# First batch's running sums added by broadcast from its third tile on; the short tile's parts in nine blocks; padding and zeros off GpSimd

## The chip, the cores and the metric

The kernel runs on one core of a Trainium2 chip. TensorE (PE), VectorE (DVE), ScalarE (ACT) and GpSimd (POOL) each run their own instruction list in order; SyncE (SP) and POOL also issue transfers. The metric is the device time of one execution in microseconds (us), as the median of several runs. Tiles of 128 rows live in on-chip memory (SBUF); PE writes into eight banks of accumulators (PSUM).

## The reference, cut to what matters

```
def _attn_ref(q, k, v, s):            # 4 batches, 8 heads, 576 tokens, head size 64
    scores = scale * np.matmul(q, k.transpose(0, 1, 3, 2))
    cum = np.cumsum(np.maximum(s, 0.0), axis=-1)
    bias = -(cum[:, :, :, None] - cum[:, :, None, :])
    scores = np.where(causal, -1e9, scores + np.minimum(bias, 0.0))
    scores = scores - np.max(scores, axis=-1, keepdims=True)
    attn = np.exp(scores)
    attn = attn / (np.sum(attn, axis=-1, keepdims=True) + 1e-09)
    return np.matmul(attn, v)

x = attention, as 2304 tokens x 512
h = x @ w1_in;  x = (h * tanh(softplus(h))) @ w1_out      # 512 -> 2048 -> 512
h = x @ w2_in;  out = (h * sigmoid(1.702 * h)) @ w2_out
```

In a row of scores the part of the bias that belongs to the query is a constant, which the softmax removes. What has to be added to a score is the running sum `cum` of its key.

## The kernel before, in words

**Work.** Each batch of 576 tokens is cut into five query tiles: `i` = 0 to 3 with 128 rows and the short tile `i` = 4 with 64. A step (`steps`, 26 of each batch, 104 in all) makes the scores of one tile for a few heads: four heads for `i` = 0, two for `i` = 1, one for `i` = 2 (width `L` = 384) and `i` = 3 (512). In the short tile a step takes two heads, one in each half of the 128 rows, and cuts its 576 columns into two pieces of 288. The eight heads are in two groups `g` of four. While attention goes on, PE also works off the first layer (`h`, 256 tokens at a time): `first_layer` calls `tick` between its products, and each `tick` emits one step. The first layer for 256 tokens can begin when their attention is done; so there are stretches in which PE has only attention to do.

**Scores and sums.** `do_qk` makes a step's scores on PE in a tile `s`, two products for each head (q split in two parts `qw`, against `kw`) and one with a mask. In batches 1 to 3 the sums come from `ck` (tiles of 128 rows, all four heads of a group; filled by `load_ck` from `cum_d` in memory, the same line to every row, in two pieces) or, for the short tile, from `ckp` (named `cp`, filled by `load_ckp` into the same buffer as `ck`). `do_max` adds them on DVE while it takes the row minimum and leaves the result in `P`; `do_exp` is the exponential on ACT, from `P` to `P`. In batch 0 the sums come by PE: one product more for each head and piece, of a one-hot matrix `oneh` and the sums in three bf16 parts `cumb`; then `early_soft` takes the minimum on DVE straight from `s` and ACT does the exponential from `s`. `cum_split` makes the columns of `cumb`.

**Attention times v.** In batches 1 to 3 `do_hilo` splits `P` into two f16 parts in a tile `hl` (three buffers) which a transposing transfer on SP's queue turns into `pt`, and `do_av` multiplies block by block, two products for each block of 128 keys (the first part against both parts of v, the second part against the first part of v). The short tile has 576 columns, so that its fifth block has 64 keys; `do_hilo` fills it up to 128 with zeros by a POOL memset, and there are ten blocks to transpose. In batch 0 `early_pt` and `early_av` do the same on PE in f32.

**Preparing.** `load_group` (transfers issued by POOL) brings k, q and v of the next group as `kraw`, `qraw`, `vraw`; ACT makes a second copy of k and q (`twice`); `qT`, `kT`, `v1` and `v2` of `split_items` make `qw`, `kw` and v's two parts. The short tile's `qw` must be zero in half its columns: POOL's memset of the whole tile does that, once its buffer (two of them) is no longer read by PE. At the start SP fetches the sixteen pieces of `w1_in` (`fetch_a`, tiles `wst`), which `turn_w` splits later with ACT, DVE and POOL.

**Order.** The code's order is a request; a scheduler decides each engine's list from its own estimates, so a change in one place can move instructions elsewhere. Within a list nothing overtakes. All arithmetic helpers pass through line 76, so the trace is read by tile names.

Of the kernel before, what the change touches and what calls it, by code (L numbers as in the profile page):

```python
# [89 lines left out]
def attention_moe_moe_kernel(  # L90
# [118 lines left out]
    def load_group(b, i, g, dup=True):  # L209
        n = min(128, S - 128 * i)  # L210
        r = []
        for src, nm in ((k, "kraw"), (q, "qraw"), (v, "vraw")):
            if nm == "vraw" and b == 0:
                v_load(i, g, nc.gpsimd)
                continue
            w = 1 if nm == "vraw" else 2
            t = pp.tile([128, HG, w, D], F32, tag=nm, name=nm, bufs=2 if nm == "qraw" else 3)
            held(nc.gpsimd.dma_start(out=t[:n, :, 0, :], in_=rows(src, b, i, g)))
            if w == 1:
                t = t[:, :, 0, :]  # L220
            elif dup:
                twice(t, n)
            r.append(t)
        raw[b, i, g] = r
# [31 lines left out]
    def split_items(b, i, g):  # L256
# [13 lines left out]
        def qT():  # L270
# [5 lines left out]
            if pair:  # L276
                nc.gpsimd.memset(w.bitcast(F32), 0.0)
# [8 lines left out]
        def v1():  # L286
            if b not in vsc:
                vscale_set(b)
            vr = raw[b, i, g][2]
            vt[b, i, g] = vv = v_p.tile([128, HG, 2, D], F16, tag="v", name="v")  # L290
            nc.scalar.activation(out=vv[:n, :, 0, :], in_=vr[:n], func=AF.Copy, scale=vsc[b][:n, 0:1])

        def v2():
            vv = vt[b, i, g]
            nc.vector.scalar_tensor_tensor(
                out=vv[:n, :, 1, :], in0=raw.pop((b, i, g))[2][:n], scalar=vsc[b][:n, 0:1], in1=vv[:n, :, 0, :],
                op0=ALU.mult, op1=ALU.subtract,
            )
# [146 lines left out]
    def early_soft(x):  # L445
# [5 lines left out]
        sg = segs(x)  # L451
        if len(sg) == 1:
            ps = x["S"][0]
            low(mx[:, 0:mu], ps[:, 0:mu * L].rearrange("p (e l) -> p e l", e=mu))
            for e in range(mu):
                o = slice(e * L, (e + 1) * L)
                lut(
                    p[:, o], ps[:, o], AF.Exp, bias=mx[:, e:e + 1], scale=-1.0, accum_out=ts["sums"][:, j + e, 0:1]
                )
            return  # L460
        for f, (c0, c1) in enumerate(sg):
            low(mx[:, f:f + 1], x["S"][f][:, 0:c1 - c0])
        low(mx[:, 2:3], mx[:, 0:2])
        sm = sm_p.tile([128, 2], F32, tag="sm2", name="sm2")
        for f, (c0, c1) in enumerate(sg):
            lut(
                p[:, c0:c1], x["S"][f][:, 0:c1 - c0], AF.Exp, bias=mx[:, 2:3], scale=-1.0, accum_out=sm[:, f:f + 1]
            )
        nc.vector.tensor_reduce(out=ts["sums"][:, j, 0:1], in_=sm, axis=mybir.AxisListType.X, op=ALU.add)
# [44 lines left out]
    def do_qk(x):  # L514
        b, i, g, n, L = x["b"], x["i"], x["g"], x["n"], x["L"]
        x["S"] = []
        for c0, c1 in segs(x):
            ps = ps_s.tile([128, 512], F32, tag="s", name="s")
            x["S"].append(ps)
            for e, hs in enumerate(x["hs"]):  # L520
                o = ps[:, e * L:e * L + c1 - c0]
                for a, h in enumerate(hs):
# [6 lines left out]
                    if b == 0:  # L529
                        m = n if len(hs) == 2 else 128  # L530
                        nc.tensor.matmul(
                            out=o[64 * a:64 * a + m], lhsT=oneh[:, h:h + 1].to_broadcast([128, m]),
                            rhs=cumb[:, c0:c1], start=False, stop=c1 < L, skip_group_check=True,
                        )
# [31 lines left out]
    def do_hilo(x):  # L566
        L, mu, nb = x["L"], x["mu"], x["nb"]
        Lp = nb * 128
        w = mu * Lp
        hl = pp.tile([128, 2 * NTIL * 128], F16, tag="hl", name="hl", bufs=HLB)  # L570
        hv = hl[:, 0:2 * w].rearrange("p (a w) -> p a w", a=2)
        if Lp != L:
            nc.gpsimd.memset(hv[:, :, L:Lp], 0.0)
        wl = mu * L
        nc.scalar.activation(out=hv[:, 0, 0:wl], in_=x["P"][:, 0:wl], func=AF.Copy, scale=PSC)
        nc.vector.scalar_tensor_tensor(
            out=hv[:, 1, 0:wl], in0=x["P"][:, 0:wl], scalar=PSC, in1=hv[:, 0, 0:wl], op0=ALU.mult, op1=ALU.subtract
        )
        x["T"] = d = pt_p.tile([128, 2 * NTIL, 128], F16, tag="pt", name="pt")
        last_pt[0] = nc.sync.dma_start_transpose(out=d[:, 0:2 * mu * nb, :], in_=hl[:, 0:2 * w])  # L580
# [4 lines left out]
    def do_av(x):  # L585
        b, i, g, n, mu, nb = x["b"], x["i"], x["g"], x["n"], x["mu"], x["nb"]
        t = x["T"]
        for e, hs in enumerate(x["hs"]):
# [5 lines left out]
            for kb in range(i + 1):  # L594
                kn = min(128, S - 128 * kb)
                for a, h in enumerate(hs):
                    hl = h - g * HG
                    rows = slice(64 * a, 64 * a + n) if two else slice(0, 128)
                    vv = vt[b, kb, g][:kn, hl, :, :].rearrange("p c d -> p (c d)")
# [4 lines left out]
                    nc.tensor.matmul(  # L604
                        out=o[rows, j % 4, 0:D], lhsT=t[:kn, (mu + e) * nb + kb, rows], rhs=vv[:, 0:D],
                        start=False, stop=(kb == i), skip_group_check=True,
                    )
# [79 lines left out]
    def tick():  # L687
# [15 lines left out]
        if t < NS:  # L703
            do_qk(x)
            if x["b"]:
                do_max(x)
                do_exp(x)
            else:
                early_soft(x)
            if last_of[gi] == t and gi in late_k:  # L710
                late_k.pop(gi)()
            if last_of[gi] == t and x["i"] == LK // 128 - 1 and x["b"]:
# [135 lines left out]
    while fq:  # L848
        fetch_a()
    early_turn(0, 0)  # L850
# [11 lines left out]
    cum_split(256, S)  # L862
# [564 lines left out]
```

## Time and profile before

| | |
|---|---|
| median of 3 runs (lowest, highest) | 1020.62 us (1016.22, 1021.12) |
| the profiled execution: its own time, its span | 1023.25 us, 1021.2 us |
| PE busy | 981.8 us, 96% of the span |
| DVE, ACT, POOL busy | 668.9, 552.7, 269.4 us |
| batch 0 | until about 133 us |
| batches 1 to 3 | until about 415 us |
| the rest (second half of layer one, layer two) | until the end |

The profile is one execution; its times are in microseconds from the start of the span. "Clock" is the share of TensorE's full speed that was granted: 1.0 is 2.4 GHz, 0.5 is 1.2 GHz. A row of the timeline gives the start, the duration, and in brackets the idle time ahead of it with what ended it. A matmul's duration includes its way through the array, so that neighbours overlap: what a matmul costs is read from one start to the next.

### The profile page before, as it was taken

To read this page: it belongs to the slowest core of one execution; us is meant where nothing else is said; L and a number is where in the kernel's file an instruction comes from. 1 tells how busy PE (TensorE), PEld (TensorE's weight loads), DVE (VectorE), ACT (ScalarE), POOL (GpSimd) and SP (SyncE) were. 2 spreads that over 40 slices of the span, in tenths; PEclk is the share of its full clock that TensorE was granted. 3 is DMA by queue.
4 is the path that set the end of the run, shared out by engine and by line. 5 is a ranking of instruction groups with operands and counts; after the bars stand their busy time and mean duration, and the time that the engine had idled before them with its cause. 6 is when DMAs were issued, how large, how long until landed. Compare 5 with 4: busy or idle time off the path is not lost.

```text
span 1021.2 us, 20117 instructions
## 1 busy us (share of the span) xinstructions
PE 981.8 (96%) x7967; PEld 870.5 (85%) x7970; DVE 668.9 (66%) x1323; ACT 552.7 (54%) x1070; POOL 269.4 (26%) x332
## 2 busy tenths in 40 slices
PE   6899999989998999999999999999999999999997
PEld 5787797978987888998888888988888888888886
DVE  5777567666465787487997995994643653653553
ACT  4675377666565887387655763753433433433331
POOL 3543332234113311000000000054434333243331
PEclk9798999999999999999999999999999999999999
DMA  9644258999589979799997553400100100000000
GB/s 260 203 127 119 74 129 159 234 209 177 132 191 199 210 146 189 238 337 357 369 336 267 181 202 134 159 8 1 63 22 1 42 22 2 22 22 1 21 9 34
DMA packets 153773, 143.16 MB, mean 140 GB/s; under 512 B 91216, under 2 KB 122448, under 8 KB 153680
## 3 DMA queue, kind: packets, MB, share of 16 engines
q1 hardware_dynamic: 147456, 124.05, 45.0%
q0 software_dynamic: 6224, 17.83, 6.6%
q8 instruction: 62, 1.02, 0.4%
q14 instruction: 31, 0.25, 0.1%
HBM read 89.61 MB, written 32.58 MB: 120 GB/s over the span
## 4 chain that ended last, share of the span: by engine, by line
PE 63%; DMA 2%; DVE 1%; ACT 0%; issue 0%; DVEq 0%; SPq 0%
PE acc L76 24%; PE h L76 21%; PE p L76 16%; DMA pt<-hl 2%; PE s L76 1%; PE o L76 1%; DVE w2l L76 0%; PE xt L76 0%; PE qt L76 0%; PE kt L76 0%; DVE z L76 0%; DVE w2d L76 0%; DVE o L76 0%; DVE f L76 0%; ACT P L76 0%
## 5 line engine op out<-in xcount | busy, mean ns | idle before, releaser
L76 PE MATMUL h<-x,w2i 128*128 128x256 f16 x1728 | 199.9, 273 | 0.9 <-DVE z L76 0.9
L76 PE MATMUL h<-xh,w 128*128 128x256 f32 x1344 | 197.3, 296 | 1.5 <-ACT xh L76 1.0
L76 PEld LDWEIGHTS <-w2i 128*128 128x128 f16 x1728 | 169.1, 98 | 20.6 <-issue 1.1
L76 PE MATMUL acc<-gh,w 128*128 128x512 f32 (+1 forms) x640 | 181.7, 369 | 0.0
L76 PEld LDWEIGHTS h<-xh,w 128*128 128x128 f32 x1344 | 174.3, 196 | 5.5 <-ACT xh L76 1.9
L76 PE MATMUL p<-w2l,gh 128*128 128x256 f16 x504 | 136.0, 273 | 0.0
L76 PE MATMUL p<-w2h,gl 128*128 128x256 f16 x504 | 135.9, 273 | 0.0
L76 PEld LDWEIGHTS acc<-gh,w 128*128 128x128 f32 x640 | 116.1, 189 | 20.4
L76 PE MATMUL p<-w2h,gh 128*128 128x256 f16 x504 | 133.3, 273 | 0.2 <-DVE e L76 0.2
L76 PE MATMUL acc<-gl,w 128*128 128x512 f32 (+1 forms) x320 | 117.9, 369 | 0.0
L76 POOL TENSOR_TENSOR s<-z 128x256 f32<-128x256 f32 x72 | 56.4, 805 | 214.2 <-DVE z L76 214.2
L76 DVE TENSOR_TENSOR gl<-z,gh 128x1024 fp32r<-128x1024 f32 (+1 forms) x72 | 94.5, 1314 | 26.2 <-ACT gh L76 25.5
L76 PEld LDWEIGHTS <-gh 128*128 128x128 f16 x1008 | 98.6, 98 | 11.8 <-issue 0.3
L76 ACT ACTIVATE sg<-h,spx 128x512 f32<-128x512 f32 x72 | 48.9, 680 | 109.7 <-PE h L76 109.7
L76 DVE SCALAR_TENSOR_TENSOR z<-h,sg 128x512 f32<-128x512 f32 x72 | 49.5, 687 | 71.5 <-ACT sg L76 71.5
L76 DVE TENSOR_TENSOR gl<-s,gh 128x1024 f16<-128x1024 f32 x36 | 44.4, 1232 | 65.4 <-ACT gh L76 65.4
L76 ACT ACTIVATE gh<-s 128x1024 f16<-128x1024 f32 x36 | 38.0, 1057 | 82.6 <-POOL s L76 82.6
L76 ACT ACTIVATE gh<-z 128x1024 fp32r<-128x1024 f32 (+1 forms) x72 | 67.9, 947 | 26.6 <-DVE z L76 24.3
L76 PE MATMUL s<-kw,qw 128*128 128x288 f32 (+4 forms) x352 | 81.3, 337 | 0.2
L76 ACT ACTIVATE P<-P,mx 128x128 f32<-128x128 f32 (+4 forms) x108 | 62.6, 580 | 21.9 <-DVE mx L76 21.3
L76 DVE CUSTOM_DVE_ANT_0 P<-s,ck 128x128 f32<-128x128 f32 (+3 forms) x96 | 44.6, 486 | 38.1 <-PE s L76 31.1
L76 PEld LDWEIGHTS acc<-gl,w 128*128 128x128 f32 x320 | 60.4, 189 | 10.2
(145 smaller groups left out, 1658.6 us busy)
## 6 DMA issues: line engine op xcount, KB each, us to landing
h_d<-hs SPq DMA_DIRECT2D x36, 512.0 KB, 4.2
hg<-h_d SPq DMA_DIRECT2D x36, 512.0 KB, 6.6
wst<-in_moe_w_in_dram SPq DMA_DIRECT2D x32, 512.0 KB, 7.7
wst<-in_moe_w_out_dram SPq DMA_DIRECT2D x32, 512.0 KB, 5.7
ck<-cum_d SPq DMA_DIRECT2D x6, 768.0 KB, 8.2
x_d<-x SPq DMA_DIRECT2D x18, 256.0 KB, 3.9
out_dram<-o SPq DMA_DIRECT2D x9, 512.0 KB, 2.8
kraw<-in_k_dram POOLq DMA_DIRECT2D x32, 128.0 KB, 4.4
```

The source lines that it names most:

```text
L76: r = f(*a, **kw)
```

## The change

- From batch 0's third tile (`i` = 2) on, no one-hot products: `do_max` and `do_exp` serve all batches in `tick`. `load_ck(0, 0)` and `load_ck(0, 1)` are issued at the start, ahead of the last three pieces of `w1_in`. `load_ckp` now runs in batch 0 too, and `load_ck` of batch 1 moves from the end of batch 0's tile 3 to the end of its tile 4, as in the other batches. The second `cum_split` goes.
- The short tile's two parts in batches 1 to 3 go in nine blocks: the 64 last columns of both parts share one block, against a copy of v's last 64 rows in both halves (a second transfer for each such `vraw`). One product does the fifth block. The second part is written by two DVE instructions instead of one; the zeros in `hl` go.
- The zeros of the short tile's `qw` are written by DVE, two memsets of half the tile's columns.

```
@@ load_group
             held(nc.gpsimd.dma_start(out=t[:n, :, 0, :], in_=rows(src, b, i, g)))
+            if w == 1 and n < 128:
+                nc.gpsimd.dma_start(out=t[n:2 * n, :, 0, :], in_=rows(src, b, i, g))
@@ split_items
             if pair:
-                nc.gpsimd.memset(w.bitcast(F32), 0.0)
+                wz = w.bitcast(F32)
+                nc.vector.memset(wz[:, 0:2, :, 64:128], 0.0)
+                nc.vector.memset(wz[:, 2:4, :, 0:64], 0.0)
@@ do_qk
-                    if b == 0:
-                        m = n if len(hs) == 2 else 128
-                        nc.tensor.matmul(
-                            out=o[64 * a:64 * a + m], lhsT=oneh[:, h:h + 1].to_broadcast([128, m]),
-                            rhs=cumb[:, c0:c1], start=False, stop=c1 < L, skip_group_check=True,
-                        )
@@ do_hilo
-        if Lp != L:
-            nc.gpsimd.memset(hv[:, :, L:Lp], 0.0)
...
+        body = w // 128 * 128
+        for c0, c1, o in ((0, body, 2 * w - body), (body, w, w)):
+            if c0 < c1:
+                nc.vector.scalar_tensor_tensor(
+                    out=hl[:, o:o + c1 - c0], in0=p[:, c0:c1], scalar=PSC, in1=hl[:, c0:c1],
+                    op0=ALU.mult, op1=ALU.subtract,
+                )
@@ do_av
-                        out=o[rows, j % 4, :], lhsT=t[:kn, e * nb + kb, rows], rhs=vv,
-                        start=(kb == 0 and j % 4 == 0), stop=False, skip_group_check=True,
+                        out=o[rows, j % 4, :], lhsT=t[:, e * nb + kb, rows], rhs=vv,
+                        start=(kb == 0 and j % 4 == 0), stop=kn < 128, skip_group_check=True,
...
+                    if kn == 128:
@@ tick
             do_qk(x)
-            if x["b"]:
-                do_max(x)
-                do_exp(x)
-            else:
-                early_soft(x)
+            do_max(x)
+            do_exp(x)
...
-            if last_of[gi] == t and x["i"] == NTIL - 1 - (x["b"] == 0) and x["b"] + 1 < B:
+            if last_of[gi] == t and x["i"] == NTIL - 1 and x["b"] + 1 < B:
                 load_ck(x["b"] + 1, x["g"])
@@ the start
     while fq:
         fetch_a()
+        if len(fq) == 3:
+            load_ck(0, 0)
+            load_ck(0, 1)
...
-    cum_split(256, S)
```

What the change does to the engines' lists is shown at three places.

On PE, the end of the first step of batch 0's short tile (`s` the scores, `qt` a transposed q for the next batch, `o` attention times v, `pt` transposed `P`). Before (ahead of these rows the first three of them stand three times more):

```order
L76 MATMUL s<-kw_480,qw 128x288 x2
L76 LDWEIGHTS oneh
L76 MATMUL s<-cumb,oneh 64x288
L76 LDWEIGHTS identb
L76 MATMUL s<-maskp,identb 128x64
L76 MATMUL qt<-ident,qraw 128x128 x4
L76 MATMUL o<-v,p_1253 128x64 x4
L76 MATMUL pt<-ident,P 128x128 x4
```

After:

```order
L76 MATMUL s<-kw_481,qw 128x288 x8
L76 LDWEIGHTS identb
L76 MATMUL s<-maskp,identb 128x64
L76 MATMUL qt<-ident,qraw 128x128 x4
L76 MATMUL o<-v,p_1240 128x64 x4
L76 MATMUL pt<-ident,P 128x128 x4
```

The four one-hot products of the step are gone, and the eight score products stand in a row; the work behind them is the same.

On SP, the transfers from the fetch of `w1_in` to the first transposes (`h_d` is the first layer's result on its way to memory, `vl` a pass over v for its scale). Before:

```order
L76 DMA wst<-in_moe_w_in_dram 128x4x256 x16
L76 DMA h_d<-hs 128x4x256 x2
L76 DMA vl<-in_v_dram 128x768 x3
L76 DMA h_d<-hs 128x4x256
L76 DMA ck_1064<-cum_d 128x4x128
L76 DMA ck_1064<-cum_d 128x4x384
L76 DMA ck_1241<-cum_d 128x4x128
L76 DMA ck_1241<-cum_d 128x4x384
L76 DMA h_d<-hs 128x4x256 x2
L76 DMA_TRANSPOSE pt<-hl 128x8x128 x2
```

After (`ck_188` and `ck_191` are batch 0's, `ck_1346` the first of batch 1's):

```order
L76 DMA wst<-in_moe_w_in_dram 128x4x256 x13
L76 DMA ck_188<-cum_d 128x4x128
L76 DMA ck_188<-cum_d 128x4x384
L76 DMA ck_191<-cum_d 128x4x128
L76 DMA ck_191<-cum_d 128x4x384
L76 DMA wst<-in_moe_w_in_dram 128x4x256 x3
L76 DMA h_d<-hs 128x4x256 x2
L76 DMA vl<-in_v_dram 128x768 x3
L76 DMA h_d<-hs 128x4x256
L76 DMA cp_1054<-cum_d 64x1152 x2
L76 DMA cp_1228<-cum_d 64x1152 x2
L76 DMA h_d<-hs 128x4x256
```

Four transfers for batch 0's sums have come into the fetch, four for its short tile stand where batch 1's stood, and batch 1's follow one `h_d` later, right ahead of the first transposes.

On POOL, the loads around batch 1's short tile. Before:

```order
L76 MEMSET qw 128x1024
L76 MEMSET hl 128x2x64
L76 DMA vraw<-in_v_dram 128x4x64 x2
L76 MEMSET hl 128x2x64
L76 DMA qraw<-in_q_dram 128x4x64
L76 MEMSET hl 128x2x64
L76 DMA kraw<-in_k_dram 128x4x64
L76 MEMSET hl 128x2x64
L76 DMA qraw<-in_q_dram 128x4x64
L76 TENSOR_TENSOR x<-x,rs 128x512
```

After:

```order
L76 DMA qraw<-in_q_dram 128x4x64
L76 TENSOR_TENSOR x<-x,rs 128x512
L76 DMA kraw<-in_k_dram 128x4x64
L76 DMA qraw<-in_q_dram 128x4x64
L76 DMA vraw<-in_v_dram 128x4x64 x2
L76 DMA kraw<-in_k_dram 128x4x64
L76 DMA qraw<-in_q_dram 128x4x64
L76 TENSOR_TENSOR x<-x,rs 128x512
```

The memsets that stood between the loads are gone.

## Rows read from the trace of the kernel before

**Rows 1.** Busy time by stretch: length, engines (with counts), granted clock, DMA share, GB/s.
```profile
50.00:107.90 57.90, 54.54 (x404) 47.37 (x406) 39.34 (x77) 33.74 (x82) 25.52 (x27) 0.94 0.38 110
107.90:126.50 18.60, 18.47 (x138) 12.88 (x136) 10.98 (x30) 8.02 (x26) 6.98 (x10) 1.00 0.35 100
```

**Rows 2.** PE's timeline, batch 0, a step of the third tile and what follows.
```profile
61.75 0.52 PE L76 MATMUL s<-kw,qw 128*128 128x384 f32 x2
62.34 0.61 PE L76 MATMUL qt<-ident,qraw 128*128 128x128 f32 x4
```

**Rows 3.** PE's timeline, batch 1, the same step and what follows.
```profile
170.55 0.52 PE L76 MATMUL s<-kw,qw 128*128 128x384 f32 x2
170.97 0.42 PE L76 MATMUL o<-v,pt 128*128 128x128 f16 x6
```

**Rows 4.** PE's timeline, batch 0, a step of the fourth tile.
```profile
80.50 0.71 PE L76 MATMUL s<-kw,qw 128*128 128x512 f32 x2
81.31 0.96 PE L76 MATMUL h<-xh,w 128*128 128x256 f32 x6
```

**Rows 5.** PE's timeline, batch 1, the same step.
```profile
195.88 0.63 PE L76 MATMUL s<-kw,qw 128*128 128x512 f32 x2
196.42 0.50 PE L76 MATMUL o<-v,pt 128*128 128x128 f16 x8
```

**Rows 6.** PE's timeline, batch 0, a step of the short tile.
```profile
107.91 0.51 PE L76 MATMUL s<-kw,qw 128*128 128x288 f32 x2
108.35 0.31 PE L76 MATMUL s<-cumb,oneh 128*64 128x288 bf16 x1
108.59 0.53 PE L76 MATMUL s<-kw,qw 128*128 128x288 f32 x2
...
110.73 0.53 PE L76 MATMUL qt<-ident,qraw 128*128 128x128 f32 x3
```

**Rows 7.** PE's timeline, batch 1, the same step.
```profile
200.19 1.22 PE L76 MATMUL s<-kw,qw 128*128 128x288 f32 x8
201.30 0.72 PE L76 MATMUL h<-xh,w 128*128 128x256 f32 x4
```

**Rows 8.** The chain that ended last, in order of time, a short tile's products.
```profile
409.21 0.68 PE o L76 x20
```

**Rows 9.** Groups by form: busy us, mean ns of one, then idle ahead and releaser.
```profile
L76 POOL MEMSET qw<- 128x1024 f32 x8 | 7.6, 954 | 45.3 <-PE s L76 40.6 <-ACT kw L76 4.5
L76 POOL MEMSET hl<- 128x128 f16 x12 | 2.4, 204 | 25.3 <-DMA pt<-hl 24.5 <-issue 0.8
L76 DVE CUSTOM_DVE_ANT_0 P<-s,ck 128x512 f32<-128x512 f32 x24 | 16.5, 686 | 10.9 <-PE s L76 10.8
L76 DVE TENSOR_REDUCE mx<-s 128x1 f32<-128x512 f32 x8 | 5.5, 681 | 2.4 <-PE s L76 2.4
```

**Rows 10.** DMA issues: KB each, median us from issue to landing.
```profile
ck<-cum_d SPq DMA_DIRECT2D x6, 768.0 KB, 8.2
```

**Rows 11.** Timeline, SP's issue of the fetch.
```profile
9.15 23.00 SPq L76 DMA_DIRECT2D wst<-in_moe_w_in_dram  x16
```

**Rows 12.** Timeline of all engines, batch 0, around the longest idle time of PE.
```profile
83.83 3.07 SPq L76 DMA_DIRECT2D ck<-cum_d  x4
94.92 0.42 ACT L76 ACTIVATE kraw<-kraw 128x256 f32<-128x256 f32 x1 [2.83 <-DMA kraw<-in_k_dram]
96.06 1.12 PE L76 MATMUL pt<-ident,P 128*128 128x128 f32 x4 [2.08 <-ACT P L76]
```

**Rows 13.** Busy time by stretch, behind that idle time (columns as in rows 1).
```profile
98.00:102.00 4.00, 3.75 (x16) 3.21 (x17) 1.12 (x2) 0.78 (x2) 0.23 (x1) 0.50 0.02 4
```

**Rows 14.** Timeline of all engines, from batch 1 to batch 2.
```profile
219.07 0.66 PE L76 MATMUL kt<-ident,kraw 128*128 128x128 f32 x4 [1.58 <-DVE qw L76]
227.01 0.29 DVE L76 CUSTOM_DVE_ANT_0 P<-s,ck 128x128 f32<-128x128 f32 x1 [3.96 <-DMA ck<-cum_d]
228.05 0.63 PE L76 MATMUL qt<-ident,qraw 128*128 128x128 f32 x4 [1.09 <-ACT P L76]
```

More of the change, by code (lines that the diff above doesn't have):

```diff
@@ L290, in v1 @@
             vt[b, i, g] = vv = v_p.tile([128, HG, 2, D], F16, tag="v", name="v")
-            nc.scalar.activation(out=vv[:n, :, 0, :], in_=vr[:n], func=AF.Copy, scale=vsc[b][:n, 0:1])
+            nc.scalar.activation(out=vv[:, :, 0, :], in_=vr, func=AF.Copy, scale=vsc[b][:, 0:1])
         def v2():
@@ L295, in v2 @@
             nc.vector.scalar_tensor_tensor(
-                out=vv[:n, :, 1, :], in0=raw.pop((b, i, g))[2][:n], scalar=vsc[b][:n, 0:1], in1=vv[:n, :, 0, :],
+                out=vv[:, :, 1, :], in0=raw.pop((b, i, g))[2], scalar=vsc[b][:, 0:1], in1=vv[:, :, 0, :],
                 op0=ALU.mult, op1=ALU.subtract,
@@ L450, in early_soft @@
         low = lambda o, i_: nc.vector.tensor_reduce(out=o, in_=i_, axis=mybir.AxisListType.X, op=ALU.min)
[L451 to L458, printed above, removed]
-                )
[L460 to L469, printed above, removed]
+        ps = x["S"][0]
+        low(mx[:, 0:mu], ps[:, 0:mu * L].rearrange("p (e l) -> p e l", e=mu))
+        for e in range(mu):
+            o = slice(e * L, (e + 1) * L)
+            lut(p[:, o], ps[:, o], AF.Exp, bias=mx[:, e:e + 1], scale=-1.0, accum_out=ts["sums"][:, j + e, 0:1])
     def early_pt(x):
@@ L567, in do_hilo @@
         L, mu, nb = x["L"], x["mu"], x["nb"]
-        Lp = nb * 128
-        w = mu * Lp
+        w = mu * L
+        nblk = 2 * w // 128
         hl = pp.tile([128, 2 * NTIL * 128], F16, tag="hl", name="hl", bufs=HLB)
-        hv = hl[:, 0:2 * w].rearrange("p (a w) -> p a w", a=2)
-        if Lp != L:
-            nc.gpsimd.memset(hv[:, :, L:Lp], 0.0)
[L574 to L578, printed above, removed]
+        p = x["P"]
+        nc.scalar.activation(out=hl[:, 0:w], in_=p[:, 0:w], func=AF.Copy, scale=PSC)
+        body = w // 128 * 128
[5 more added lines that the diff above has]
+                )
         x["T"] = d = pt_p.tile([128, 2 * NTIL, 128], F16, tag="pt", name="pt")
-        last_pt[0] = nc.sync.dma_start_transpose(out=d[:, 0:2 * mu * nb, :], in_=hl[:, 0:2 * w])
+        last_pt[0] = nc.sync.dma_start_transpose(out=d[:, 0:nblk, :], in_=hl[:, 0:2 * w])
     ohold = {}
@@ L598, in do_av @@
                     rows = slice(64 * a, 64 * a + n) if two else slice(0, 128)
-                    vv = vt[b, kb, g][:kn, hl, :, :].rearrange("p c d -> p (c d)")
+                    vv = vt[b, kb, g][:, hl, :, :].rearrange("p c d -> p (c d)")
                     nc.tensor.matmul(
-                        out=o[rows, j % 4, :], lhsT=t[:kn, e * nb + kb, rows], rhs=vv,
-                        start=(kb == 0 and j % 4 == 0), stop=False, skip_group_check=True,
-                    )
[L604 to L607, printed above, removed]
+                        out=o[rows, j % 4, :], lhsT=t[:, e * nb + kb, rows], rhs=vv,
+                        start=(kb == 0 and j % 4 == 0), stop=kn < 128, skip_group_check=True,
+                    )
+                    if kn == 128:
+                        nc.tensor.matmul(
+                            out=o[rows, j % 4, 0:D], lhsT=t[:, (mu + e) * nb + kb, rows], rhs=vv[:, 0:D],
+                            start=False, stop=(kb == i), skip_group_check=True,
+                        )
             if j % 4 == 3:
```

3 lines of the change are left out of this document (1 added, 2 removed).

## The prediction

> **What bounds the kernel now.** I read the busy time by stretch first, then PE's timeline inside the stretches, then what the other engines wait for. Until 107.9 us, with batch 0's middle tiles and the first layer mixed, PE is busy for 54.54 of 57.9 us and VectorE for 39.34; from 107.9 to 126.5, where PE has batch 0's short tile and preparing to do but almost no first layer, PE is busy for 18.47 of 18.6 and VectorE for 10.98 [rows 1]. So in batch 0 the end is set by PE's own work, and a PE instruction that goes there gives its time back, as long as no other engine comes to be the slower one. The longest single idle time of PE in this stretch is 2.08 us [rows 12]. In the later batches PE waits here and there for transposes, for ScalarE and VectorE; they are changed only at the short tile.
>
> **The one-hot products.** What a step costs on PE is read from the start of its first score product to the start of the next work, in batch 0 with the one-hot product, in batch 1 without.
> - Third tile, 8 steps: 62.34 - 61.75 = 0.59 us with [rows 2], 170.97 - 170.55 = 0.42 without [rows 3]: 0.17 x 8 = 1.36 us.
> - Fourth tile, 8 steps: 81.31 - 80.50 = 0.81 with [rows 4], 196.42 - 195.88 = 0.54 without [rows 5]: 0.27 x 8 = 2.16 us.
> - Short tile, 4 steps: 110.73 - 107.91 = 2.82 with [rows 6], 201.30 - 200.19 = 1.11 without [rows 7]: 1.71 x 4 = 6.84 us.
>
> Together 10.36 us. The short tile has only 16 of the 32 one-hot products and yet two thirds of the sum, which is worth a second look: two score products and one one-hot take 108.59 - 107.91 = 0.68 us, of which 0.44 pass until the one-hot starts and 0.24 from there [rows 6]; nine products in a row, the mask among them, take 1.11, or 0.12 each [rows 7], so that the two should take 0.24 and the one 0.12. By 0.12 for each removed product the 16 would give 1.97 us and not 6.84; the rest is the changes of form, since a one-hot here fills only half the array's columns (128*64 in its row [rows 6]).
>
> The Trainium skill ("TensorEngine Tiling (Array Packing)", Key Properties) says that a change of tiling mode drains TensorE. The rows agree: 0.20 us more ahead of each half-width product and 0.12 more behind it than products in a row need. Without that rule one would take the 0.12 as the price and come to a sum smaller by 4.9 us. The sum goes by the steps as measured, since the row of batch 1 shows the step as it will be.
>
> **The nine blocks.** A step of the short tile loses 2 of its 20 products in batches 1 to 3, 24 in all. Twenty take 0.68 us at the end of the chain, 0.034 each [rows 8], so 0.8 us; that they are half-height products between full ones may add some, at most as much again. The transposes get 9/10 of their size in 12 of 78 cases. Against this stand a VectorE instruction more in each of 12 steps (64 columns, between 0.1 and 0.3 us by the 0.68 for 512 columns [rows 9]), and six small transfers more to issue on POOL, which loses 7.6 + 2.4 us of memsets for it [rows 9]. None of that is on PE; neither engine is full.
>
> **What VectorE and ScalarE take over.** In tiles 3 and 4 the sum with minimum takes VectorE 0.686 us for 512 columns where the minimum alone took 0.681 [rows 9]; for 16 steps that is nothing. The memsets for `qw` are new there: no row has one on VectorE. Bounds: POOL's 0.204 us for 128 columns and 0.954 for 1024 [rows 9]; I take 0.3 for 256 columns, 16 of them, 4.8 us in all, three quarters of it in batches 1 to 3. In the list each pair stands right ahead of the `P` of the group's last step, which waits for nearly the same score products of PE as the memset does for its buffer, so behind it nothing is held up for longer than its own 0.6 us. The second `cum_split`, 5 instructions of VectorE at the start, goes; the work behind it waited for PE's scores anyway: nothing.
>
> **The moved transfers.** Each broadcast of a group is 1 MB; its larger piece lands 8.2 us after its issue [rows 10], and four pieces take SP 3.07 us to issue [rows 12]. SP issues the sixteen pieces of `w1_in` from 9.15 us on in 23.00, 1.44 each [rows 11], so the new broadcasts come behind the thirteenth at about 28 us and have landed at about 28 + 3.1 + 8.2 = 39; a step of the third tile, their first reader, is at work at 61.75 [rows 2], the first of these eight perhaps ten earlier. The last three pieces of `w1_in` come later by up to 11 us; they are the last of sixteen that the first layer uses, and with 3 of 16 still to go it is well past 61.75. Both at nothing; if the cover were gone, each could cost what it is late, up to 11 us. The short tile's `cp` is issued after its group's last use of `ck`, two steps or more ahead of its own; nothing.
>
> **Sum.** 10.36 + 0.8 = 11.2 us off the profiled execution's 1023.25, so 1012.1. That execution stands 2.6 above the median; the same off 1020.62 gives **1009.5 us** for the median.
>
> **Rivals.**
> *More than the sum (A).* PE's 2.08 us of idle time at 94 us came from ScalarE, which stood 2.83 us for a `kraw` that had not landed, after four broadcasts for batch 1 had been issued from 83.83 us on [rows 12]; behind the idle time PE ran at half clock, 0.50 from 98 to 102 [rows 13]. The change takes these broadcasts and POOL's memset away from there. If the stall goes, that is 2.1 us and another 2 from the clock in these 4 us alone. Further, POOL's `hl` memsets wait 24.5 us for transposes [rows 9] with loads of k and q queued behind them; earlier loads there could give 1 to 3 us at the two batch ends behind. Together 5 to 7 us more: about 1003.5. Against: broadcasts of batch 1 still come, some 25 us later, and can hit other loads.
>
> *The gain is given back, no change (B).* From 107.9 to 126.5 PE's work falls from 18.5 to 11.7 us, and VectorE's stays at 11 [rows 1]: both would be full, and a chain from scores over minimum, exponential and transposes to products has no first layer to fill its gaps. If VectorE with its waits needs 14 us, 2.3 us of the gain are gone. Then, from batch 0 to batch 1, the broadcast of batch 1 now comes late, as from batch 1 to 2 before: there VectorE waited 3.96 us for `ck`, and PE 1.58 + 1.09 us behind it and what was late before it [rows 14]. With two half-clock stretches as at 98 (2 us each for 4 us at 0.50 [rows 13]) that is 2.3 + 2.7 + 4 = 9 us: about 1018.5.
>
> The Trainium skill ("TensorE: Matmul & The Clock Gate", Part 1) says that the clock is set by how busy PE was before. That speaks against a change which thins PE's work out where a chain sets the pace, and is why B counts two such stretches; the trace agrees once, at 98 us, and PE's other idle times show that it doesn't follow each.
>
> *Slower (C).* The same late broadcast alone, at the step that begins batch 1: VectorE stands at `ck`, with the second parts of `hl` and so the transposes and PE's products queued behind. To come out over 1025.7, PE would have to lose 11.2 + 5.1 = 16.3 us there. From batch 1 to 2 a wait of 3.96 cost 2.7 [rows 14]; it would take a wait of some 20 us, and the piece that lands slowest needs 8.2 [rows 10], with two short-tile steps of 3.1 us or more between issue and use. If the list on SP were held by a first-layer result (one `h_d` now stands ahead of batch 1's broadcasts) it could happen.
>
> **Chances.** What can be told from no change here is about 0.5%, 5.1 us. The sum, within 4 us of 1009.5: 0.52. A, below 1005.5: 0.24. B, from 1013.5 up to 1020 or so: 0.20. C: 0.04. Two fifths of B lie under 1015.5, so faster 0.84, same 0.12, slower 0.04. The range reaches from A's 1002 to 1017.5, into B, and leaves about 0.08 out on the fast side and 0.12 on the slow one.
>
> **What the next profile would show.** Right: steps of batch 0's short tile at 1.1 us from first score to next work; PE still over 95% busy until batch 0's end; batch 1's first scores some 10 us earlier than before. A: no idle time of 2 us and no half clock between 90 and 105 us. B: idle time of PE behind ScalarE's `P` in the short tile, VectorE waiting for `ck` at the start of batch 1, half clock near either. It would be wrong if PE were as busy as before in batch 0 and the time had gone elsewhere, or if idle time appeared in batches 1 to 3, whose lists are sorted anew.

## The result, and the profile of the changed kernel

| | before | changed |
|---|---|---|
| median of 13 runs each (lowest, highest) | 1020.52 us (1016.22, 1024.06) | 1009.41 us (1007.33, 1017.47) |
| the profiled execution: its own time, its span | 1023.25, 1021.2 us | 1012.26, 1010.5 us |
| PE busy | 981.8 us | 969.2 us |
| DVE, ACT, POOL busy | 668.9, 552.7, 269.4 us | 671.1, 553.9, 264.6 us |

The ratio is 0.991, with a 95% interval of 0.9887 to 0.9933: 9.2 us less, between 6.8 and 11.5. The medians stand 11.1 us apart, the spans 10.7, and PE's busy time fell by 12.6.

Busy time by stretch of the changed kernel, for the stretches that answer to [rows 1] (length, PE, weight loads, VectorE, ScalarE, GpSimd with counts, granted clock, DMA share, GB/s), and behind them the place of the old stall [rows 12, 13]:

```profile
50.00:104.70 54.70, 50.17 (x395) 44.04 (x396) 43.99 (x100) 37.09 (x87) 25.82 (x28) 1.00 0.33 92
104.70:123.00 18.30, 18.06 (x170) 16.61 (x170) 13.08 (x41) 10.89 (x28) 6.72 (x9) 1.00 0.75 225
94.00:99.00 5.00, 4.84 (x37) 3.90 (x37) 5.00 (x12) 4.00 (x10) 1.78 (x2) 1.00 0.62 126
```

The second row holds all of batch 0's short tile and ends with batch 1's first scores: 18.3 us, where the same way took 24.5 before (from 107.91 [rows 6] to 132.39). PE is idle for 0.24 us in it, and VectorE is far from full. At 94 us there is no stall and the clock is whole. But the first row shows 4.5 us of idle PE where [rows 1] shows 3.4.

PE's timeline of the changed kernel: the first step of the third tile, a step of the fourth, one of the short tile, and batch 1's first scores:

```profile
54.80 0.62 PE L76 MATMUL s<-kw,qw 128*128 128x384 f32 x2 [0.45 <-DVE kw L76]
...
92.67 0.63 PE L76 MATMUL s<-kw,qw 128*128 128x512 f32 x2
93.14 0.23 PE L76 MATMUL s<-maskb,identb 128*128 128x128 bf16 x1
93.21 0.61 PE L76 MATMUL pt<-ident,P 128*128 128x128 f32 x4
...
104.71 1.29 PE L76 MATMUL s<-kw,qw 128*128 128x288 f32 x8
105.84 0.20 PE L76 MATMUL s<-maskp,identb 128*128 128x64 bf16 x1
105.88 0.63 PE L76 MATMUL qt<-ident,qraw 128*128 128x128 f32 x4
...
123.02 0.34 PE L76 MATMUL s<-kw,qw 128*128 128x128 f32 x2
```

The step of the fourth tile takes 93.21 - 92.67 = 0.54 us [0.81 in rows 4], that of the short tile 105.88 - 104.71 = 1.17 [2.82 in rows 6]. The third tile, however, begins at 54.80 us and not at 50.43 as before: PE's list now has 62 `h` products ahead of the first `kt` instead of 38, because ScalarE's list has its first copies of `kraw` and `qraw` behind two more splits of `w`. So 4.4 us are lost by then, and batch 1 still begins 9.4 us earlier.

In batches 1 to 3: PE's longest idle time, and its two single runs of eighteen products at the end (timeline). Behind them two of PE's waits over the whole execution (engine, what it did, for whom; us in all, times, longest), and the same two in the kernel before:

```profile
227.73 0.82 PE L76 MATMUL o<-v,pt 128*128 128x128 f16 x8 [6.90 <-DMA pt<-hl]
...
399.37 0.60 PE L76 MATMUL o<-v,pt 128*64 128x128 f16 x18 [0.60 <-DMA pt<-hl]
399.90 2.30 PE L76 MATMUL h<-xh,w 128*128 128x256 f32 x17
403.09 0.60 PE L76 MATMUL o<-v,pt 128*64 128x128 f16 x18
403.62 3.61 PE L76 MATMUL acc<-xh,w 128*128 128x256 f32 x28
```

```profile
PE o L76 <- DMA pt<-hl: 14.1, 11, 6.9
PE pt L76 <- ACT P L76: 1.8, 3, 1.2
```

```profile
PE o L76 <- DMA pt<-hl: 11.1, 8, 2.4
PE pt L76 <- ACT P L76: 3.5, 3, 2.1
```

The waits for `P` all lie in batch 0; those of the changed kernel end at 27, 30 and 70 us, ahead of the short tile.

And the groups by form that answer to [rows 9] (busy us, mean ns, idle ahead and its releaser):

```profile
L76 DVE CUSTOM_DVE_ANT_0 P<-s,ck 128x512 f32<-128x512 f32 x32 | 21.6, 675 | 8.7 <-PE s L76 5.9 <-PE o L76 2.6
L76 DVE CUSTOM_DVE_ANT_0 P<-s,ck 128x128 f32<-128x128 f32 x24 | 5.6, 287 | 4.6 <-PE s L76 2.3 <-DMA ck<-cum_d 1.8 <-PE o L76 0.4
L76 DVE MEMSET qw<- 128x256 f32 x16 | 4.4, 272 | 2.1 <-PE s L76 2.0
```

A run of eighteen takes 0.53 us, against 0.68 for twenty [rows 8]. VectorE waits for `ck` for 1.8 us in all and the zeros take it 0.27 us each. New against the kernel before is the idle time of 6.90 us at the change from batch 1 to batch 2. Behind it PE runs at a lower clock, and again 100 us later:

```profile
224.00:231.00 7.00, 3.27 (x20) 3.08 (x21) 2.35 (x8) 3.63 (x10) 0.79 (x1) 0.57 0.99 204
324.00:327.30 3.30, 3.30 (x30) 2.86 (x29) 2.62 (x11) 3.27 (x14) 1.08 (x2) 0.50 1.09 321
```

### The profile page after: what moved, and what is told of

The parts are those of the page before. It is cut to its first block, busy times and chain, and to the rows that moved or that the text cites. A ratio compares the mean times of both kernels' runs of the same rounds, so it can differ in the third digit from the quotient of the medians.

```text
span 1010.5 us, 20045 instructions
## 1 busy us (share of the span) xinstructions
PE 969.2 (96%) x7914; PEld 863.8 (85%) x7914; DVE 671.1 (66%) x1362; ACT 553.9 (55%) x1062; POOL 264.6 (26%) x318
## 4 chain that ended last, share of the span: by engine, by line
PE 64%; DMA 3%; DVE 1%; issue 1%; POOL 0%; ACT 0%; DVEq 0%; SPq 0%; POOLq 0%
PE acc L76 24%; PE h L76 21%; PE p L76 16%; DMA pt<-hl 2%; PE s L76 1%; DMA qraw<-in_q_dram 1%; PE o L76 1%; DVE w2l L76 0%; PE kt L76 0%; PE qt L76 0%; DVE z L76 0%; DVE w2d L76 0%; PE xt L76 0%; DVE hl L76 0%; DVE o L76 0%
## 5 line engine op out<-in xcount | busy, mean ns | idle before, releaser
L76 ACT ACTIVATE P<-P,mx 128x384 f32<-128x384 f32 (+4 forms) x128 | 76.2, 596 | 29.4 <-DVE mx L76 28.6
L76 PE MATMUL s<-kw,qw 128*128 128x288 f32 (+4 forms) x352 | 77.6, 331 | 0.4 <-DVE kw L76 0.4
L76 DVE CUSTOM_DVE_ANT_0 P<-s,ck 128x384 f32<-128x384 f32 (+3 forms) x112 | 54.2, 503 | 30.5 <-PE s L76 24.3
```

Of the source, the lines that this page charges most:

```text
L76: r = f(*a, **kw)
```

## The experiments

Theory: in batch 0 PE's own work sets the time, the half-width one-hot products cost it mostly by the change of form, and the other two parts of the change weigh little. Rivals: the gain comes from the stall that vanished at 94 us; or from GpSimd, whose memsets no longer stand ahead of loads; or a one-hot product costs only its columns, and the sum is right by chance.

All the times, each group against the kernel before on the same chip (difference: 1 less the ratio, times the median of before, with the interval's ends):

| kernel | median us | before | ratio (95%) | difference us |
|---|---|---|---|---|
| broadcasts alone | 1009.93 | 1019.18 | 0.9908 (0.9877 to 0.9940) | -9.4 (-12.5 to -6.1) |
| nine blocks alone | 1017.42 | 1019.18 | 0.9968 (0.9938 to 0.9998) | -3.3 (-6.3 to -0.2) |
| changed, short tile with one-hot | 1017.44 | 1019.18 | 0.9980 (0.9954 to 1.0005) | -2.0 (-4.7 to +0.5) |
| before, one-hot over the full width | 1014.12 | 1019.18 | 0.9953 (0.9930 to 0.9975) | -4.8 (-7.1 to -2.5) |
| zeros on VectorE alone | 1023.10 | 1019.53 | 1.0031 (1.0007 to 1.0055) | +3.2 (+0.7 to +5.6) |
| changed, copies first | 1008.78 | 1019.53 | 0.9888 (0.9848 to 0.9927) | -11.4 (-15.5 to -7.4) |
| changed, `h_d` from ScalarE's queue | 1010.71 | 1019.53 | 0.9905 (0.9874 to 0.9935) | -9.7 (-12.8 to -6.6) |
| changed, both of these | 1010.16 | 1019.53 | 0.9897 (0.9863 to 0.9932) | -10.5 (-14.0 to -6.9) |
| the changed kernel once more | 1011.52 | 1021.65 | 0.9908 (0.9885 to 0.9931) | -9.4 (-11.7 to -7.0) |
| changed, zeros on GpSimd | 1006.13 | 1021.65 | 0.9865 (0.9843 to 0.9886) | -13.8 (-16.0 to -11.6) |
| changed, zeros on GpSimd, copies first | 1004.35 | 1021.65 | 0.9844 (0.9819 to 0.9868) | -15.9 (-18.5 to -13.5) |

The twelfth, ten full-height blocks, was run once (1019.15 us) to read one row of it.

And the stretch of batches 1 to 3 by itself, from the first scores of batch 1 to the first `acc` of layer one's second half, in one profiled execution each:

| kernel | begins | length | PE busy | clock |
|---|---|---|---|---|
| before | 132.39 | 280.57 | 263.85 | 0.99 |
| broadcasts alone | 122.63 | 279.23 | 264.11 | 0.98 |
| nine blocks alone | 129.12 | 276.22 | 262.09 | 0.99 |
| zeros on VectorE alone | 127.84 | 284.81 | 265.68 | 0.98 |
| changed | 123.02 | 279.02 | 262.36 | 0.98 |
| changed, once more | 123.42 | 275.14 | 260.79 | 0.99 |
| changed, copies first | 119.24 | 282.45 | 263.08 | 0.98 |
| changed, zeros on GpSimd | 121.41 | 274.01 | 260.24 | 1.00 |
| changed, zeros on GpSimd, copies first | 119.18 | 274.95 | 260.00 | 1.00 |

Read in pieces of half a microsecond, these stretches hold between none and 14 us at half clock: 7.0 us before, 14.0 with the broadcasts alone, 7.0 with nine blocks, 14.0 with the zeros on VectorE, 10.5 and 3.5 in the two executions of the changed kernel, 10.0 with the copies first, none in the last two rows.

### Each part alone: the broadcasts

The kernel before with these lines, and the one-hot products of `do_qk` and the second `cum_split` gone:

```
+        if len(fq) == 3:
+            load_ck(0, 0)
+            load_ck(0, 1)
...
-            if x["b"]:
-                do_max(x)
-                do_exp(x)
-            else:
-                early_soft(x)
+            do_max(x)
+            do_exp(x)
...
-            if last_of[gi] == t and x["i"] == LK // 128 - 1 and x["b"]:
+            if last_of[gi] == t and x["i"] == LK // 128 - 1:
...
-            if last_of[gi] == t and x["i"] == NTIL - 1 - (x["b"] == 0) and x["b"] + 1 < B:
+            if last_of[gi] == t and x["i"] == NTIL - 1 and x["b"] + 1 < B:
```

> The kernel before with the broadcasts alone (no one-hot products from the third tile on, broadcasts of batch 0 in the fetch, those of batch 1 later); ten blocks with their zeros and GpSimd's memset stay. Theory, PE's own work in batch 0 sets the gain: 10.4 us less than before, about 1010.1, and PE busy about 11 us less. Rival, the gain comes from GpSimd, whose memsets no longer stand ahead of loads: this kernel keeps them all, so no more than a third of the 11.1 us, about 1017.

It is 9.4 us faster and PE is busy for 970.6 us, 11.2 less than before. This part makes about as much as the whole change; GpSimd keeps its memsets here, so they are not where the gain comes from. A long idle time at the change from batch 1 to batch 2 stands here as well, with ten blocks and GpSimd's zeros:

```profile
218.84 0.85 PE L76 MATMUL o<-v,pt 128*64 128x128 f16 x15 [6.57 <-DMA pt<-hl]
```

The kernel with the full-width product (below), whose batches 1 to 3 have no part of the change, waits 4.47 us for a transpose at this change of batches. So such an idle time needs neither the nine blocks nor the zeros on VectorE.

### Each part alone: nine blocks

`do_hilo`, `do_av`, the second transfer of `vraw` and the full 128 rows of `v1` and `v2` as in the change, nothing else.

> The kernel before with nine blocks alone for the short tile's parts in batches 1 to 3. Theory: 24 products of 0.034 us, 0.8 us less, about 1019.7, not to be told from no change. Rival, the zeros that waited 24.5 us on GpSimd for transposes held up loads that PE waits for: 3 to 5 us less, about 1016.5, with less idle time of PE at the two batch ends.

3.3 us less, with an interval from 0.2 to 6.3, which decides between neither. The trace shows the part of PE's work: PE is busy for 976.8 us, 5.0 less, 1.8 of it in batches 1 to 3 (263.85 to 262.09), where the products were taken out. The other 3.2 lie mostly in batch 0, which this edit leaves alone: there the kernel before ran at half clock from 96 to 102.5 us and this one did not. PE's idle time in batches 1 to 3 is 2.6 us smaller too (14.1 us and 16.7), about what two executions of the changed kernel differ by (16.7 and 14.4), so that the rival of earlier loads is neither shown nor excluded. 1.8 us is more than twice the 0.8 of the theory; the last experiment takes it apart.

### Each part alone: the zeros on VectorE

```
-                nc.gpsimd.memset(w.bitcast(F32), 0.0)
+                wz = w.bitcast(F32)
+                nc.vector.memset(wz[:, 0:2, :, 64:128], 0.0)
+                nc.vector.memset(wz[:, 2:4, :, 0:64], 0.0)
```

> The kernel before, the zeros of the short tile's qw by VectorE in two instructions instead of GpSimd, nothing else. Theory, none of it is on PE and neither engine is full: no change, 1019 to 1021. Rival, GpSimd's memset waited up to 45 us for PE with loads behind it, and those loads are what PE waits for: 3 us less or more, about 1016.5.

Neither: it is 3.2 us slower, and the interval excludes no change. Batch 1 begins 4.6 us earlier than before, but batches 1 to 3 take 4.2 us longer, and the end is later. PE's waits there, from the list of waits of this kernel:

```profile
PE o L76 <- DMA pt<-hl: 9.4, 9, 2.2
...
PE qt L76 <- ACT qraw L76: 3.3, 2, 3.0
PE qt L76 <- ACT kw L76: 3.3, 1, 3.3
PE kt L76 <- DVE qw L76: 1.7, 2, 1.3
```

The two waits of 3 us, both where a batch ends, are longer than any of these before [rows 14]. The mean clock over whole executions is no lower than before, 0.9859 in its twelve runs and 0.9854 in the 22 of the kernel before on the same chip, so a lower clock does not account for the 3.2 us; in the one execution read, half clock went from batch 0 and came in batches 1 to 3. The parts add up: -9.4 - 3.3 + 3.2 = -9.5 us, and the changed kernel stands at -9.2 and -9.4; each of the three has an interval of 2 to 3 us to either side, so this is a weak test.

### The price of a half-width product

The changed kernel, with the short tile's one-hot products, its minimum and exponential straight from the scores, and the second `cum_split` put back:

```
+                    if b == 0 and i == NTIL - 1:
+                        m = n if len(hs) == 2 else 128
+                        nc.tensor.matmul(
+                            out=o[64 * a:64 * a + m], lhsT=oneh[:, h:h + 1].to_broadcast([128, m]),
+                            rhs=cumb[:, c0:c1], start=False, stop=c1 < L, skip_group_check=True,
+                        )
```

> The changed kernel, but the short tile of batch 0 keeps its one-hot products and its minimum straight from the scores; all transfers but the four for its sums stand as in the changed kernel. Theory, each of the four steps costs PE 1.71 us more with half-width one-hot products: 6.8 us more than the changed kernel, about 1016.2. Rival, a product costs the 0.12 us of its columns and no more: 2 us more, about 1011.4. Rival, the stall at 94 us and the half clock behind it made the gain, and the moved broadcasts took it away: as the changed kernel, 1009.4 to 1010.

It stands at 0.9980 of before where the changed kernel stands at 0.9910: 0.0070 x 1019 = 7.1 us slower, against 6.8 expected; both intervals together leave some 3.5 us to either side, which excludes the 2 us of the price by columns. The stall at 94 us is away in both, so this difference does not come from it. A step from its first scores to the next work:

```profile
107.48 0.50 PE L76 MATMUL s<-kw,qw 128*128 128x288 f32 x2
...
110.30 0.64 PE L76 MATMUL kt<-ident,kraw 128*128 128x128 f32 x4
```

2.82 us again. Batch 1 begins at 127.73 us, 4.7 later than in the changed kernel; the rest of the 7.1 is not placed by single executions.

And the other way, the kernel before with both heads of the short tile in one product over all 128 columns:

```
-                    if b == 0:
-                        m = n if len(hs) == 2 else 128
-                        nc.tensor.matmul(
-                            out=o[64 * a:64 * a + m], lhsT=oneh[:, h:h + 1].to_broadcast([128, m]),
-                            rhs=cumb[:, c0:c1], ...
+                    if b == 0 and a == len(hs) - 1:
+                        w1h = oneh[:, h:h + 1].to_broadcast([128, 128])
+                        if len(hs) == 2:
+                            w1h = onew[:, 2 * (h // 4) + h % 2]
+                        nc.tensor.matmul(out=o, lhsT=w1h, rhs=cumb[:, c0:c1], ...
```

(`onew` holds, for each pair of heads, the one head's column 64 times and then the other's; GpSimd makes it at the start.)

> The kernel before, its short tile in batch 0 with one one-hot product for both heads over the full 128 columns, in place of two over 64; two such products in a step instead of four, the rest as before, the broadcast of batch 1 and the stall at 94 us too. Theory, the price is the change of form: a step of 2.82 us goes to 1.11 + 2 x 0.12 = 1.35 us, 5.9 us less in four steps, about 1014.6. Rival, the price goes with the number of products, 1.71 / 4 = 0.43 us each: 1.97 us a step, 3.4 us less, about 1017.1. Rival, only the columns cost: 8 x 0.12 = 1 us less, about 1019.5.

A step in PE's timeline:

```profile
107.54 0.77 PE L76 MATMUL s<-kw,qw 128*128 128x288 f32 x4
108.15 0.30 PE L76 MATMUL s<-cumb,onew 128*128 128x288 bf16 x1
108.19 0.79 PE L76 MATMUL s<-kw,qw 128*128 128x288 f32 x4
108.83 0.30 PE L76 MATMUL s<-cumb,onew 128*128 128x288 bf16 x1
108.96 0.19 PE L76 MATMUL s<-maskp,identb 128*128 128x64 bf16 x1
108.99 0.63 PE L76 MATMUL qt<-ident,qraw 128*128 128x128 f32 x4
```

108.99 - 107.54 = 1.45 us; the theory said 1.35, the price by number 1.97, before it was 2.82 [rows 6]. Four steps of 1.37 less are 5.5 us. Batch 1 begins at 126.88 us, 5.5 earlier than before, with no broadcast in batch 0, with an idle time of 1.83 us at 95 and with half clock behind it as before. The kernel is 4.8 us faster. By their number the two products that went would have taken 0.86 us a step with them; what went beyond that is the half width itself. This one edit is half of what the whole change brings.

### The idle times that came with the new lists

In the changed kernel, ScalarE's first four copies of `kraw` and `qraw` ahead of its next split of `w`:

```
+        copies.append(held(nc.scalar.activation(out=t[:n, :, 1, :], in_=t[:n, :, 0, :], func=AF.Copy)))
...
+        hi = nc.scalar.activation(out=th, in_=y, func=AF.Copy)
+        for c in copies[0:4]:
+            tc.add_manual_dep(hi.ins, c.ins.name, order, reason="copies first")
```

> The changed kernel, with ScalarE's four first copies of kraw and qraw put ahead of its next split of w, as in the list of before. In the changed kernel they stand two splits later, PE does 62 h products ahead of its first kt where it did 38, and the third tile's first scores come at 54.80 us instead of 50.43. Theory, this gave back 4 us of what the lost stall at 94 us had saved: first scores of the third tile at 50 or earlier, batch 1 begins 4 us earlier, about 1005.5. Rival, PE is full in batch 0 and the order of its products is all one, the idle time only moves: as the changed kernel, 1009 to 1010.

The third tile's first scores come at 50.56 us and batch 1 begins at 119.24, 3.8 us earlier, as the theory has it. But batches 1 to 3 take 3.4 us more than in the changed kernel (282.45 and 279.02), and the ratios, 0.9888 and 0.9910, don't tell the two apart. So the later third tile does cost 4 us until batch 1; at the end of this kernel they don't show for certain.

The first layer's results by ScalarE's queue:

```
-            nc.sync.dma_start(
+            nc.scalar.dma_start(
                 out=h_d[:, m:m + 4, u * U:(u + 1) * U], in_=t.rearrange("p (m t) -> p m t", m=4)
```

> The changed kernel, with the first layer's results sent to memory from ScalarE's queue, right behind the copy that makes them, instead of from SP's. In the changed kernel PE's longest idle time, 6.90 us at 227.73, is for a transpose that stood behind such a transfer on SP, and that for ScalarE. Theory, the place in SP's queue is the cause: this idle time falls to 4 us or less and no half clock stands behind it, 3 to 5 us less than the changed kernel, about 1005.5. Rival, the transposes are slow for the other transfers that share the engines with them: the idle time stays, and ScalarE loses 0.4 us of issue 36 times, so no gain or up to 3 us more, 1009 to 1012.

The long idle time is gone, yet PE waits as long for transposes in all (first row of its waits):

```profile
PE o L76 <- DMA pt<-hl: 14.1, 10, 3.0
```

14.1 us in ten waits where the changed kernel has 14.1 in eleven. That fits the theory that the place in SP's queue made the one long wait, but two executions of one kernel differ there by 2.4 us (below). Half clock still stands behind the longest wait of now, from 225 to 228.5 us, and lasts 14 us in batches 1 to 3. No gain shows.

> The two edits before this one together on the changed kernel: ScalarE's copies first, and the first layer's results from ScalarE's queue. If both theories hold, their sums add: 8 us less than the changed kernel, about 1001.5. If only one holds, about 1005.5; if the rivals hold, 1009 to 1012.

-10.5 us, no different from either. With the zeros on VectorE neither edit shows a gain.

### The three parts put together otherwise

> The changed kernel as it is, beside the two below, and as a second execution in which to read PE's idle times of batches 1 to 3. The same time as before it, 1009.4 within 3 us. If the idle time of 6.90 us at 227.73 us belongs to the order of the lists, it stands there again within 1 us; if it is one execution's accident of the transfers, it is under 4 us or elsewhere.

-9.4 us again. PE's longest wait is at the same place in the list, but 4.51 us long:

```profile
225.52 0.60 PE L76 MATMUL o<-v,pt 128*128 128x128 f16 x8 [4.51 <-DMA pt<-hl]
```

That lies between the two marks: the place belongs to the lists, the size differs by 2.4 us between two executions. The whole stretch of batches 1 to 3 is 3.9 us shorter in this execution (275.14 and 279.02), so in the table above a difference of less than that says nothing by itself, the 3.4 us after the copies among them.

The changed kernel with GpSimd's one memset for the zeros of `qw`:

```
-                wz = w.bitcast(F32)
-                nc.vector.memset(wz[:, 0:2, :, 64:128], 0.0)
-                nc.vector.memset(wz[:, 2:4, :, 0:64], 0.0)
+                nc.gpsimd.memset(w.bitcast(F32), 0.0)
```

> The changed kernel with the zeros of the short tile's qw given back to GpSimd's one memset; broadcasts and nine blocks stay. Theory, the three parts add: the zeros on VectorE cost 3.2 us by themselves, so without them the changed kernel is 2 to 4 us faster, about 1006.5. Rival, the zeros cost nothing and the 3.2 us were lists that fell otherwise: as the changed kernel, 1009 to 1010.

It is faster than the changed kernel: 0.9865 (0.9843 to 0.9886) beside 0.9908 (0.9885 to 0.9931) on the same chip, 4.4 us, with some 3 us to either side. The parts without the zeros add to -9.4 - 3.3 = -12.7, and it stands at -13.8. Its waits for transposes:

```profile
PE o L76 <- DMA pt<-hl: 7.4, 9, 2.1
```

They are shorter than the 14.1 and 11.0 us of the changed kernel's two executions, but the fastest kernel, the next one, has 11.2 again, so they do not explain the times by themselves. The clock says more: over the whole execution it lies at 0.991 to 0.994 in these six runs, 0.9923 in the mean, and at 0.985 to 0.992 in the six of the changed kernel beside them, 0.9885. As it has two levels, that is 2 x 0.0038 x 1009 = 7.7 us less at half clock, and if PE was at work throughout, half of that is won: 3.8 us, an estimate. So most of the 4.4 us can be time at half clock, whereas the zeros alone brought no more of that than there was before.

And with the copies first too:

> As the kernel before this one (zeros by GpSimd), with ScalarE's four first copies of kraw and qraw ahead of its next split of w too. Theory, the 3.8 us that these gain until batch 1 stay when VectorE has no zeros to write: about 1003. Rival, batches 1 to 3 end when their transfers let them (DMA share 0.89 to 0.91 there), so a batch 0 that ends earlier is waited for later: as the kernel before this one.

-15.9 us, the fastest of all, 6.5 us below the changed kernel beside it. Batch 1 begins 2.2 us earlier than in the kernel before this one, and 1.8 us of median are kept; the intervals of the two overlap, so this last step is not shown.

### Twenty full-height products

The kernel before, with the fifth block of the short tile over all 128 rows; the transposed zeros meet v's copy:

```
-                    vv = vt[b, kb, g][:kn, hl, :, :].rearrange("p c d -> p (c d)")
+                    vv = vt[b, kb, g][:, hl, :, :].rearrange("p c d -> p (c d)")
...
-                        out=o[rows, j % 4, :], lhsT=t[:kn, e * nb + kb, rows], rhs=vv,
+                        out=o[rows, j % 4, :], lhsT=t[:, e * nb + kb, rows], rhs=vv,
```

> The kernel before with ten blocks and all twenty products in the short tile of batches 1 to 3, the two of the fifth block over all 128 rows (their lower half zeros times a second copy of v) instead of 64. Read: the run of twenty products, 0.68 us before, and of eighteen, 0.53 us in the changed kernel. Theory, half-height products among full ones cost more than their number: the twenty take 20 x 0.53 / 18 = 0.59 us. Rival, only the number counts: they stay at 0.66 to 0.68 us.

PE's timeline at the end of its batch 3:

```profile
405.44 0.63 PE L76 MATMUL o<-v,pt 128*64 128x128 f16 x20
406.00 0.44 PE L76 MATMUL xt<-ident,x 128*128 128x128 f32 x2
...
409.71 0.63 PE L76 MATMUL o<-v,pt 128*64 128x128 f16 x20
410.27 4.10 PE L76 MATMUL acc<-xh,w 128*128 128x256 f32 x32
```

The twenty take 0.56 us, less even than 0.59. Of the 0.15 us that a step wins by nine blocks, 0.12 are the half-height products and 0.03 the two products fewer.

## Why the prediction came out right, point by point

**The bound.** Right: PE's own work in batch 0 set the time. PE stays full in the short tile, and the broadcasts alone bring 9.4 us of the 10.4 expected. That batch 1 begins 9.4 us earlier is in part the clock of the one execution of the kernel before that was read: the 6.5 us at 0.50 from 96 to 102.5 us cost it about 3 us (an estimate, half of them). Two kernels with the same steps in batch 0 had the same idle time there, 2.04 us (nine blocks) and 2.05 (full height), kept the whole clock behind it, and begin batch 1 at 129.12 and 127.89 us. Against these the changed kernel begins it 4.9 to 6.1 us earlier, about the 10.4 less the 4.4 by which its third tile is late.

**The one-hot products.** Right in size and cause for the short tile: 1.17 us a step for 1.11, 7.1 us in the whole kernel for 6.84, and 1.45 where only the form was changed. The Trainium skill ("TensorEngine Tiling (Array Packing)", Key Properties) says that a change of tiling mode drains TensorE; the traces agree in both directions, columns (2.82 us to 1.45 with full-width products, of which fewer products explain at most 0.86) and rows (0.68 to 0.56 with full-height ones). No run separates such a drain from another price of a half-width product itself.

**The nine blocks.** The mechanism was right and the size off: 0.8 us was worked out as 24 products by 0.034, with "at most as much again" for the half-height ones. It is 12 x 0.15 = 1.8 us, and 1.8 less of busy PE, mostly the half height, which alone costs 12 x 0.12 = 1.4 us against that bound of 0.8; the time says 3.3, with an interval that holds 1.8.

**The zeros on VectorE.** This step failed. "Behind it nothing is held up for longer than its own 0.6 us" gave nothing for them; 0.27 us for one was estimated well (0.3), but the kernel with them is slower by 3.2 us when they stand alone and by 4.4 in the changed one. As far as single executions tell, the loss lies in batches 1 to 3: with nine blocks these take 276.22, 274.01 and 274.95 us with the zeros on GpSimd, and 279.02, 275.14 and 282.45 with them on VectorE. The cause stays open. The two losses are not made alike: alone, the mean clock of whole executions stays as it was, and PE waits for `qraw` and `kw` where a batch ends; in the changed kernel most of the loss can be half clock. The longest idle time of the changed kernel needs no zeros on VectorE, since the broadcasts alone have 6.57 us there. Whether VectorE's 4.4 us themselves cost the time or the lists that were sorted anew around them was not separated.

**The sum.** 11.2 us was expected for the median and 11.1 came; by the ratio 9.2. Two steps were wrong with opposite signs: nine blocks bring 1 us or more beyond what was put down, and the zeros cost 3 to 4 that were put down at nothing. Two more that the sum left out stand against each other, the late third tile and the stall with its half clock that went. So the price of the one-hot products was understood, and that the whole sum came out so close is luck.

**Rival A** was half right. The stall at 94 us and its half clock vanished, as it said, but the third tile came 4.4 us later. The price of that lateness is shown until batch 1 (copies first: 3.8 us); its cause is in ScalarE's list. The prediction asked only when the moved transfers land and put them at nothing; the lists that came with them cost this, for the third tile is as late with the broadcasts alone (54.44 us). How much of the vanished half clock reached the end was not separated, but it may be a part of the gain: over whole executions the mean clock is 0.9862 before and 0.9882 with the broadcasts alone on one chip, 0.9840 and 0.9885 (changed) on another, which by the estimate above is worth up to 2.0 us and 4.6 us.

**Rival B** did not come: no wait behind ScalarE's `P` in the short tile, and VectorE waits for `ck` once, 1.8 us at 212.7 us, not at the start of batch 1; before it was twice, 3.96 [rows 14] and 1.53. What the prediction named as a sign of being wrong, idle time in batches 1 to 3, did come (6.90 us), but in all PE stands idle there as long as before, 16.7 us in both. The two stretches at a lower clock exist, 224 and 324 us, but the kernel before had two such as well, besides the one at 98 us that the prediction knew (0.50 from 178 to 181 and from 239.5 to 242.5 us), and they stand behind waits for transposes and for `qraw`. **Rival C** found no place: VectorE does not wait for batch 1's broadcasts.

## What to carry to other kernels

A small product in another form than its neighbours is priced by what passes from the start of the one ahead to the start of the one behind, in its own trace and in a stretch without it, not by its columns; here filling the array with a second head cost 0.17 us a product instead of 0.43. Split a change into its parts before keeping it all: here one part cost 3 to 4 us while the sum still looked like the plan. Where a scheduler writes the lists, an instruction that moves to an engine with room to spare is not free for that: look at the waits at every stage's end after it moved. And before a few microseconds are put down to an edit, compare the granted clock of the runs on both sides.

## What the runs showed of the hardware that was not expected

- Half-width one-hot products of 288 columns among full-width ones cost 1.71 us for the four of a step, 0.43 each; full-width ones 0.17 each ((1.45 - 1.11) / 2).
- Four products of half height among twenty cost 0.12 us more than the same over all rows.
- VectorE's sum with minimum of 512 columns takes 0.675 us in the changed kernel, no more than the 0.681 of the minimum alone [rows 9].
- The wait for the same transpose was 6.90 us in one execution and 4.51 in another of the same kernel.
- Behind an idle time of 2.08 us of PE in batch 0 the clock was 0.50 for 6.5 us; behind 2.04 and 2.05 us at the same place, in executions of two other kernels, it stayed at 1.00:

```profile
96.00:102.50 6.50, 6.19 (x26) 5.65 (x28) 1.81 (x3) 2.31 (x7) 1.29 (x1) 0.50 0.01 3
95.00:103.00 8.00, 7.18 (x56) 6.20 (x57) 2.93 (x5) 3.55 (x10) 1.45 (x2) 1.00 0.04 11
94.00:103.00 9.00, 8.34 (x66) 7.43 (x68) 3.98 (x9) 3.95 (x12) 2.70 (x3) 1.00 0.01 4
```

These are stretches of the kernel before, of nine blocks alone and of ten full-height blocks, with columns as in [rows 1].
